# Induced attention and channel mix on one core: the product for the previous token moved onto half of the array's rows

## The chip, the cores and the metric

The kernel runs on one NeuronCore of a Trainium2 chip. The metric is the device time of one execution in microseconds (us). Three runs were taken before the change, and one execution was profiled; the profile gives the span from the first to the last instruction.

## The reference

For each of 4 batches x has 12608 tokens of 128 channels. 32 inducing vectors attend to all tokens of a batch and give h (32 x 128); each token then attends to h. What comes out passes through a channel mix with the previous token:

```python
h = mab(I, x)                # softmax(scale * I x^T) x, per batch
a = mab(x, h)                # softmax(scale * x h^T) h, per token
x_prev = shift(a, 1)         # zeros for the first token
xk = mu_k * a + (1 - mu_k) * x_prev
xr = mu_r * a + (1 - mu_r) * x_prev
k = maximum(xk @ w_k, 0)     # 128 -> 1024
v = k * k @ w_v              # 1024 -> 128
out = sigmoid(xr @ w_r) * v
```

The kernel never forms a. With p the token's 32 attention weights, a @ (mu_k w_k) is p @ (h mu_k w_k): for each batch it folds h, mu and w into two matrices, W0 for the token and W1 for the previous one, of 32 rows and 1024 + 128 columns (the last 128 for the gate w_r). Both p and W are split into a high and a low part that together keep float32's precision in a faster product type. So a row block of 32 partitions of R (p's parts) meets a row block of W0 or W1, and with two parts of each there are four combinations a matrix: 4 x 32 = 128 rows.

## The kernel before, in words

**Units.** Tokens are worked in groups g of 512, 25 a batch (24 full ones and a last of 320). The 1024 columns are eight chunks of 128, worked two at a time: a unit is one group and two chunks, so four units a group, 100 a batch, 400 in all, written as steps n of one loop. In step n the loop writes, in this order: the upward products of unit n (`up`, L773 with W0 and the tokens, L775 with W1 and the tokens shifted by one, both over 128 rows, summed in one of the two two-bank tiles ps_a); the square (`square`: relu to k_t on DVE, L785; the rounded square kh on ACT, L790, or in chosen steps, `high_vector`, on DVE, L787; the square itself on ACT, L791; their difference kl on POOL, L793); in the second unit of a group the gate (`zgate`, L762 and L763, two more products, then a sigmoid on ACT, L765); the downward products of unit n - 4 (`down`, L804: kh with wvh, kh with wvl, kl with wvh, for two chunks). When a group's last unit is done DVE multiplies by the gate (L809), transposes into the output tile ot (L820), and SP issues four stores (L827) for every four groups. ot has one buffer, so its next use waits for the stores.

**R.** R holds p's parts for one group: 128 partitions and 513 columns, column 0 being the last token of the group before. The row blocks are high, low, high, low. It has ten buffers. SP fills it in `spread` (L664): four copies within on-chip memory for a group, each of 32 partitions by 512. Before them `halo` (L587) copies the column for the token before from R of the previous group, as one transfer.

**The work between.** The rest is written into the loop's steps by `at(n, ...)`, in blocks that start every 12 steps. `stage_a(b + 1, j)` prepares the next batch: four DVE transposes of x into tiles xs (three buffers), each followed by four copies into xt on SP (L336, 16 a block), then scores against the inducing vectors (L361), exponentials and a sum (L426), and a load of x (L205). `stage_b(b, j)` makes p for a block of four groups: scores against h (L610), softmax steps on DVE and ACT over some ten steps, the parts ah on ACT (L650) and al on DVE (L654), and then in four steps the four spreads. The last block, the tail of 320 tokens, goes through the same steps with narrower copies. `combine` makes h, its four copies scaled by mu (L519), and W, whose row blocks SP copies (L565, 24 copies a batch).

**Order.** All this is written out by hand: every engine works strictly in program order, and SP too issues its DMAs in the order of the steps, waiting at each for its producers. Batch 0 differs: a head prepares it before the loop, and its first four groups' R are put directly from PSUM, by one ACT copy each (L738).

Of the kernel before, what the change touches and what calls it, by code (L numbers as in the profile page):

```python
# [19 lines left out]
def kernel(  # L20
# [15 lines left out]
    P = 128  # L36
# [8 lines left out]
    LAG = 4  # L45
    NU = FC // UC
# [9 lines left out]
    r_pool = ctx.enter_context(tc.tile_pool(name="r_pool", bufs=10))  # L56
# [23 lines left out]
    wv_sb = mp.tile([P, Q * G], F32, name="ot", bufs=1)[:, :F].rearrange("p (c d) -> p c d", d=C)  # L80

    def load_weight(dst, src, n, raw):
# [11 lines left out]
        def steps():  # L94
# [20 lines left out]
            def sign():  # L115
                X.r = st.tile([P, G], I32, name="aT")[:, :n]
                v.tensor_scalar(out=X.r, in0=hi, scalar1=-2147483648, scalar2=None, op0=ALU.bitwise_and)
# [185 lines left out]
    def xt_tile(S, j, i):  # L303
# [4 lines left out]
        elif i == 0:  # L308
            S.xt_tail = xt_pool.tile([P, TAIL], F32, name="xtl", bufs=1)
# [4 lines left out]
    def stage_a(b, j, at, t):  # L314
# [13 lines left out]
        def btr(c):  # L328
            if c == 0:
                for i in range(Q):  # L330
                    xt_tile(S, j, i)
            xs = st.tile([P, G], F32, name="xs", bufs=3)
            nc.vector.transpose(out=xs.rearrange("p (s q) -> p s q", q=M),  # L333
                                in_=S.xb[j][:, :, M * c:M * (c + 1)])
            for i in range(Q):
                nc.sync.dma_start(out=S.xt[j, i][M * c:M * (c + 1), :], in_=xs[M * i:M * (i + 1)])  # L336
# [70 lines left out]
        def t_etrans():  # L407
            ps = pb_tile("b")
# [36 lines left out]
        for c in range(Q):  # L445
            at(t + (-1, 0, 1, 3)[c], lambda c=c: btr(c))
        if tail:
            at(t + 5, t_tr)
# [20 lines left out]


    def combine(b, at=None, t=0):
# [18 lines left out]
        def weights():  # L490
# [6 lines left out]
            ps = pb_tile(None if ahead else "b")  # L497
# [12 lines left out]
        def hfin():  # L510
            ps = pb_tile(None if ahead else "b")
# [5 lines left out]
            for nm, mu in (("k0", muk), ("k1", omuk), ("r0", mur), ("r1", omur)):  # L517
                h4 = L["h4"][nm] = sm.tile([P, P], F32, name="h4" + nm, bufs=1)
                nc.vector.tensor_scalar(out=h4, in0=h, scalar1=mu, scalar2=None, op0=ALU.mult)  # L519
            S.W = [wp.tile([P, WF], F32R, name=f"W{s}") for s in range(2)]  # L520

        def wpart(s, c, tile):
# [13 lines left out]
            def low():  # L536
                nc.vector.tensor_tensor(out=dst[P // 2:], in0=X["ps"][P // 2:, :],
                                        in1=dst.bitcast(F32)[P // 2:], op=ALU.subtract)
            return prod, high, low

        def wpack(parts, cw, tags, t):
# [33 lines left out]
        at(t + 9, weights)  # L575
        at(t + 10, hfin)
# [490 lines left out]
```

## Time and profile before

| what | value |
|---|---|
| three runs | 1167.78, 1167.95 and 1170.74 us, median 1167.95 |
| the profiled execution | 1165.47 us |
| its span, first to last instruction | 1163.7 us |
| granted TensorE clock | 0.996 of full speed |
| PE, ACT, POOL, DVE busy | 96%, 83%, 81%, 80% of the span |
| DMA | 102.31 MB in 273515 packets, 40.5% of the 16 engines' time on SP's queue |

In the rows that follow, a timeline row gives the start in us, the length in us, the engine (SPq is SP issuing a DMA), the line, what is written from what, and how many instructions were merged. A row of the waits gives the waiting engine and line, whom it waited for, and then us in total, times, and the longest in us. A row of the groups gives the count, busy us, the mean in ns and idle us before. A matmul's end is modelled, so lengths of matmuls overlap: the distance between two starts is the time that one takes.

### The profile page before, as it was taken

The page shows a single profiled execution, that of the slowest core. Times are in us where ns is not written, and L with a number is a line of the kernel's source. Part 1 is how long each engine was busy: PE and PEld are TensorE (multiplying, and loading weights), DVE is VectorE, ACT ScalarE, POOL GpSimd, SP SyncE. Part 2 cuts the span into 40 slices and gives each one's busy share as a digit, 9 for nine tenths or more (in the row PEclk, how much of TensorE's full clock was granted, in tenths as well). Part 3 has the DMA queues.
Part 4 walks back from the last instruction along what each step waited for, and adds up shares of the span by engine and source line. Part 5 has one row for each costly group of instructions (what it writes and reads, how often), then busy time and mean ns, then how long its engine had stood idle before and what let it go on. Part 6 is the DMA issues. An engine that isn't in the chain of part 4 may idle for free.

```text
span 1163.7 us, 17576 instructions
## 1 busy us (share of the span) xinstructions
PE 1114.2 (96%) x5746; PEld 834.2 (72%) x5746; DVE 934.3 (80%) x1259; ACT 970.9 (83%) x1107; POOL 947.7 (81%) x413
## 2 busy tenths in 40 slices
PE   7779999999999999999999999999999999999997
PEld 5456777776677777777767777777768777777886
DVE  5778889887878888888787889897787888887665
ACT  5478888887888888788978988888789888889996
POOL 1158888888787888888879888888878899999997
PEclk9989999999999999999999999999999999999999
DMA  9112554544226455465043554645304314432231
GB/s 288 50 32 75 128 118 106 109 117 92 39 58 134 108 105 123 108 135 120 5 76 74 118 125 104 134 96 124 45 15 82 63 34 73 73 64 46 43 46 34
DMA packets 273515, 102.31 MB, mean 88 GB/s; under 512 B 232816, under 2 KB 248336, under 8 KB 271120
## 3 DMA queue, kind: packets, MB, share of 16 engines
q1 hardware_dynamic: 273088, 101.17, 40.5%
q8 instruction: 46, 0.75, 0.3%
q14 instruction: 45, 0.37, 0.1%
q10 hardware_dynamic: 336, 0.02, 0.0%
HBM read 28.07 MB, written 25.82 MB: 46 GB/s over the span
## 4 chain that ended last, share of the span: by engine, by line
PE 61%; DVE 15%; ACT 8%; SPq 6%; issue 5%; DMA 4%; DVEq 0%; ACTq 0%
PE ps_v L804 31%; PE ps_a L773 11%; PE ps_a L775 10%; DVE k_t L785 5%; SPq L336 2%; DMA out_dram<-ot 2%; ACT kh L790 2%; SPq L827 2%; PE pb_a L426 1%; PE pb_b L610 1%; PE ps_v L762 1%; PE ps_v L763 1%; SPq L664 1%; ACT k_t L791 1%; PE pb_a L361 1%
## 5 line engine op out<-in xcount | busy, mean ns | idle before, releaser
L793 POOL TENSOR_TENSOR kl<-k_t,kh 128x1024 fp32r<-128x1024 f32 (+2 forms) x400 | 939.0, 2375 | 169.0 <-ACT k_t L791 148.9
L785 DVE TENSOR_SCALAR k_t<-ps_a 128x1024 f32<-128x1024 f32 (+1 forms) x400 | 480.9, 1202 | 155.5 <-PE ps_a L775 144.1
L791 ACT ACTIVATE k_t<-k_t 128x1024 f32<-128x1024 f32 (+1 forms) x400 | 418.2, 1048 | 45.5 <-DVE kh L787 34.3
L790 ACT ACTIVATE kh<-k_t 128x1024 fp32r<-128x1024 f32 (+1 forms) x352 | 365.9, 1040 | 104.5 <-DVE k_t L785 57.8
L773 PE MATMUL ps_a<-R,W 128*128 128x512 f32 (+1 forms) x800 | 325.9, 408 | 4.7 <-DMA R<-al 3.4
L775 PE MATMUL ps_a<-R,W 128*128 128x512 f32 (+1 forms) x800 | 313.6, 392 | 0.0
L804 PE MATMUL ps_v<-kh,wvh 128*128 128x512 f32 (+1 forms) x800 | 251.9, 396 | 5.5 <-ACT rT L765 5.0
L804 PE MATMUL ps_v<-kl,wvh 128*128 128x512 f32 (+1 forms) x800 | 249.2, 393 | 0.0
L804 PE MATMUL ps_v<-kh,wvl 128*128 128x512 f32 (+1 forms) x800 | 249.0, 392 | 0.0
L773 PEld LDWEIGHTS ps_a<-R,W 128*128 128x128 f32 x800 | 151.2, 189 | 82.3 <-issue 22.4
L804 PEld LDWEIGHTS ps_v<-kh,wvh 128*128 128x128 f32 x800 | 147.9, 189 | 42.3 <-ACT rT L765 10.1
L804 PEld LDWEIGHTS ps_v<-kl,wvh 128*128 128x128 f32 x800 | 149.6, 188 | 35.5 <-POOL kl L793 0.3
L804 PEld LDWEIGHTS ps_v<-kh,wvl 128*128 128x128 f32 x800 | 149.8, 188 | 34.9
L775 PEld LDWEIGHTS ps_a<-R,W 128*128 128x128 f32 x800 | 151.1, 189 | 29.8
L820 DVE STREAM_TRANSPOSE ot<-oT 128x512 f32<-128x512 f32 x96 | 67.4, 702 | 12.2 <-DMA out_dram<-ot 11.3
L809 DVE TENSOR_TENSOR oT<-ps_v,rT 128x512 f32<-128x512 f32 (+1 forms) x100 | 66.7, 667 | 2.4 <-PE ps_v L804 0.2
L787 DVE SCALAR_TENSOR_TENSOR kh<-ps_a,k_t 128x1024 fp32r<-128x1024 f32 x48 | 58.8, 1225 | 5.4 <-PE ps_v L804 0.5
L765 ACT ACTIVATE rT<-ps_v 128x512 f32<-128x512 f32 (+1 forms) x99 | 57.2, 578 | 0.3
L333 DVE STREAM_TRANSPOSE xs<-xb 128x512 f32<-128x512 f32 x72 | 50.0, 695 | 0.3
L765 ACT ACT_TABLE_LOAD x31 | 39.8, 1283 | 0.6
L762 PE MATMUL ps_v<-R,W 128*128 128x512 f32 (+1 forms) x99 | 38.9, 393 | 0.0
L763 PE MATMUL ps_v<-R,W 128*128 128x512 f32 (+1 forms) x99 | 38.7, 391 | 0.0
(194 smaller groups left out, 643.6 us busy)
## 6 DMA issues: line engine op xcount, KB each, us to landing
out_dram<-ot SPq DMA_DIRECT2D x92, 256.0 KB, 4.4
xb<-in_x_dram SPq DMA_DIRECT2D x18, 1024.0 KB, 5.3
xt<-xs SPq DMA_DIRECT2D x288, 64.0 KB, 2.0
R<-ah SPq DMA_DIRECT2D x184, 64.0 KB, 2.0
R<-al SPq DMA_DIRECT2D x184, 64.0 KB, 2.0
kh<-in_x_dram SPq DMA_DIRECT2D x4, 512.0 KB, 8.2
kl<-in_x_dram SPq DMA_DIRECT2D x4, 512.0 KB, 6.4
xb<-in_x_dram SPq DMA_DIRECT2D x8, 256.0 KB, 5.4
```

Source lines behind the costliest of these rows:

```text
L762: nc.tensor.matmul(out=ps[:, :w], lhsT=S.W[0][:, F:WF], rhs=R[:, 1:w + 1], start=True, stop=False)
L765: nc.scalar.activation(out=self.rT, in_=ps[:, :w], func=AF.Sigmoid)
L773: nc.tensor.matmul(out=ps[:, c, :w], lhsT=S.W[0][:, cs], rhs=R[:, 1:w + 1], start=True, stop=False)
L775: nc.tensor.matmul(out=ps[:, c, :w], lhsT=S.W[1][:, cs], rhs=R[:, 0:w], start=False, stop=True)
L785: nc.vector.tensor_scalar(out=k, in0=self.ps[:, :, :w], scalar1=0.0, scalar2=None, op0=ALU.max)
L787: nc.vector.scalar_tensor_tensor(out=kh, in0=self.ps[:, :, :w], scalar=0.0, in1=k, op0=ALU.max, op1=ALU.mult)
L790: nc.scalar.activation(out=kh, in_=k, func=AF.Square)
L791: nc.scalar.activation(out=k, in_=k, func=AF.Square)
L793: return lambda eng, a, z: eng.tensor_tensor(out=kl[:, :, a:z], in0=k[:, :, a:z], in1=kh.bitcast(F32)[:, :, a:z], op=ALU.subtract)
L804: nc.tensor.matmul(out=self.v, lhsT=wt[:, fc, :], rhs=kk[:, c, :], start=(fc == 0 and n == 0), stop=(fc == FC - 1 and n == 2))
L809: nc.vector.tensor_tensor(out=self.oT, in0=self.v, in1=self.rT, op=ALU.mult)
L820: nc.vector.transpose(out=ot[:, o:o + w], in_=self.oT)
```

## The change

*Products.* One of the four combinations of parts, low with low, is left out for each of the two matrices. The six that remain need 192 rows: 128 for one full product and 64 for a second. The full product has W0's three combinations and, in its last row block, one of W1's with the high part shifted by one column; the half has W1's other two. R becomes [128, 2, 513]: plane 0 for the full product and, in its rows 0 to 63, the half for even chunks; plane 1 in rows 64 to 127 holds the same half for odd chunks. In a unit, both full products come first, then the two halves, one on rows 0 to 63 and one on rows 64 to 127, into different banks. The gate gets a full product and one half alone. Shape, type and count of the downward products stay.

*Copies.* A spread is six copies instead of four, and a halo three transfers instead of one (in the head, three DVE copies instead of one). W keeps 24 copies a batch, three for each part of W0 and five for each of W1. Of the scaled copies of h, two are whole, two cover 96 columns, and two DVE copies fill the rest. The head puts a group's R by two ACT copies and one DVE copy.

*Memory.* R has six buffers of the double width instead of ten; ot holds two groups instead of four, and stores are issued every two groups; the tail's output no longer has a tile of its own; xt of the tail has two buffers.

*Order.* From batch 1 on, blocks start every 14 steps instead of 12, stage_a of the next batch 13 steps ahead of its stage_b; in batch 0 stage_a keeps 12 steps and stage_b has steps of its own. A transpose of x and its copies may stand in different steps. The tail's softmax is written closer together. `combine` and the next batch's first stage_b keep their distances to the last stage_a block (21 and 25 steps from its start). The steps with kh on DVE move, and are 14 a batch from batch 1 on. Some small products use the other PSUM bank.

The diff, cut to its core:

```diff
-    r_pool = ctx.enter_context(tc.tile_pool(name="r_pool", bufs=10))
+    r_pool = ctx.enter_context(tc.tile_pool(name="r_pool", bufs=6))
...
         def btr(c):
+            L["xs", c] = st.tile([P, G], F32, name="xs", bufs=3)
...
+        def bmove(c):
...
             for i in range(Q):
-                nc.sync.dma_start(out=S.xt[j, i][M * c:M * (c + 1), :], in_=xs[M * i:M * (i + 1)])
+                nc.sync.dma_start(out=S.xt[j, i][M * c:M * (c + 1), :], in_=L["xs", c][M * i:M * (i + 1)])
...
-        for c in range(Q):
-            at(t + (-1, 0, 1, 3)[c], lambda c=c: btr(c))
+        for c, n in enumerate((-2, -1, 1, 3) if b > 1 else (-1, 0, 1, 3)):
+            at(t + n, lambda c=c: btr(c))
+            at(t + max(n, -1), lambda c=c: bmove(c))
...
+    W_FIRST = ((0, 0, 0), (0, 1, 0), (0, 2, 1))
+    W_SECOND = ((0, 3, 0), (1, 1, 0), (1, 3, 0), (1, 0, 1), (1, 2, 1))
+    def r_tile():
+        return r_pool.tile([P, UC, G + 1], F32R, name="R")
...
-            for nm, mu in (("k0", muk), ("k1", omuk), ("r0", mur), ("r1", omur)):
-                h4 = L["h4"][nm] = sm.tile([P, P], F32, name="h4" + nm, bufs=1)
-                nc.vector.tensor_scalar(out=h4, in0=h, scalar1=mu, scalar2=None, op0=ALU.mult)
+            for nm, mu, omu in (("k", muk, omuk), ("r", mur, omur)):
...
+                nc.vector.tensor_scalar(out=h1, in0=h, scalar1=omu, scalar2=None, op0=ALU.mult)
...
+                nc.vector.tensor_scalar(out=h0[:, :P - M], in0=h[:, :P - M], scalar1=mu, scalar2=None, op0=ALU.mult)
+                nc.vector.tensor_copy(out=h0[:, P - M:], in_=h1[:, P - M:])
...
-                for q in range(Q):
-                    nc.sync.dma_start(out=S.W[s].bitcast(F32)[M * q:M * (q + 1), c0:c0 + cw],
-                                      in_=X["hl"][q // 2][M * n:M * (n + 1)])
+                for d, q, k in (W_FIRST, W_SECOND)[s]:
+                    nc.sync.dma_start(out=S.W[d].bitcast(F32)[M * q:M * (q + 1), c0:c0 + cw],
+                                      in_=X["hl"][k][M * n:M * (n + 1)])
...
     def halo(S, g, far=True):
...
-        elif far:
-            nc.sync.dma_start(out=S.R[g].bitcast(F32)[:, 0:1], in_=S.R[g - 1].bitcast(F32)[:, G:G + 1])
+        for dst, src in ((R[:half, 0, 0:1], O[:half, 0, G:G + 1]),
+                         (R[half:, 1, 0:1], O[half:, 1, G:G + 1]),
+                         (R[P - M:, 0, 1:2], O[half:P - M, 1, G:G + 1])):
+            if far:
+                nc.sync.dma_start(out=dst, in_=src)
+            else:
+                nc.vector.tensor_copy(out=dst.bitcast(F32R), in_=src)
...
         def spread(i):
...
-            for q in range(Q):
-                nc.sync.dma_start(out=R[M * q:M * (q + 1), 1 + o + lo:1 + o + w],
-                                  in_=src[q % 2][M * i:M * (i + 1), lo:w])
+            for q, h, k, d in ((0, 0, 0, 1), (1, 0, 1, 1), (2, 0, 0, 1), (3, 0, 0, 2), (2, 1, 0, 1), (3, 1, 1, 1)):
+                z = min(w, G + 1 - d - o)
+                nc.sync.dma_start(out=R[M * q:M * (q + 1), h, d + o + lo:d + o + z],
+                                  in_=src[k][M * i:M * (i + 1), lo:z])
...
-                nc.scalar.copy(out=S.R[g][:, 1:G + 1], in_=ps)
+                nc.scalar.copy(out=R[:P - M, 0, 1:G + 1], in_=ps[:P - M])
+                nc.vector.tensor_copy(out=R[P // 2:, 1, 1:G + 1], in_=ps[P // 2:])
+                nc.scalar.copy(out=R[P - M:, 0, 2:G + 1], in_=ps[P // 2:P - M, :G - 1])
...
-            nc.tensor.matmul(out=ps[:, :w], lhsT=S.W[0][:, F:WF], rhs=R[:, 1:w + 1], start=True, stop=False)
-            nc.tensor.matmul(out=ps[:, :w], lhsT=S.W[1][:, F:WF], rhs=R[:, 0:w], start=False, stop=True)
+            nc.tensor.matmul(out=ps[:, :w], lhsT=S.W[0][:, F:WF], rhs=R[:, 0, 1:w + 1], start=True, stop=False)
+            nc.tensor.matmul(out=ps[:, :w], lhsT=S.W[1][:P // 2, F:WF], rhs=R[:P // 2, 0, 0:w],
+                             start=False, stop=True)
...
-            for c in range(UC):
-                cs = slice((u * UC + c) * P, (u * UC + c + 1) * P)
-                nc.tensor.matmul(out=ps[:, c, :w], lhsT=S.W[0][:, cs], rhs=R[:, 1:w + 1],
+            for c, cs in enumerate(cols):
+                nc.tensor.matmul(out=ps[:, c, :w], lhsT=S.W[0][:, cs], rhs=R[:, 0, 1:w + 1],
                                  start=True, stop=False)
-                nc.tensor.matmul(out=ps[:, c, :w], lhsT=S.W[1][:, cs], rhs=R[:, 0:w],
+            for c, cs in enumerate(cols):
+                rows = slice(c * P // UC, (c + 1) * P // UC)
+                nc.tensor.matmul(out=ps[:, c, :w], lhsT=S.W[1][rows, cs], rhs=R[rows, c, 0:w],
                                  start=False, stop=True)
...
-            span = 1 if self.b == B - 1 and g // Q == NBLK - 2 else Q
+            span = 1 if self.b == B - 1 and g // Q == NBLK - 2 else UO
...
-    SEG = 12
...
+        if b == 0:
+            first_a = [t + 3 + 12 * j for j in range(NBLK - 1)]
+            first_b = [t + n for n in (4, 16, 28, 40, 63, 77)]
+            high_vector |= {s + n for s in first_a for n in (4, 8)}
+        else:
+            first_a = [t - 9 + 14 * j for j in range(NBLK - 1)]
+            first_b = [t + n for n in (4, 18, 32, 46, 60, 74)]
+            high_vector |= {s + n for s in first_a for n in (7, 10)} | {t + 80, t + 90}
...
         if b + 1 < B:
-            s = t + SEG * (NBLK - 1)
-            combine(b + 1, at, s)
-            stage_b(b + 1, 0, at, s + 13)
+            s = first_a[-1]
+            combine(b + 1, at, s + 21)
+            stage_b(b + 1, 0, at, s + 25)
```

More of the change, by code (lines that the diff above doesn't have):

```diff
@@ L510, in hfin @@
         def hfin():
-            ps = pb_tile(None if ahead else "b")
+            ps = pb_tile(None if ahead else "a")
             nc.tensor.matmul(out=ps[:, :P], lhsT=S.acc, rhs=L["sw"], start=True, stop=True)
@@ L696, in scores @@
                 del S.xt[0, g]
-                S.R[g] = r_pool.tile([P, G + 1], F32R, name="R")
+                S.R[g] = r_tile()
         def diff():
@@ L838 @@
     order_a = [(b, j) for b in range(B) for j in range(NBLK)]
-    def k_tile():
-        return mp.tile([P, UC * G], F32, name="k_t", bufs=4)
     def halves():
```

98 lines of the change are left out of this document (49 added, 49 removed).

## The prediction

> **What bounds the kernel now.** I read the page first, then the timeline of PE, then that of SP, the queue that issues nearly every DMA.
>
> ```profile
> span 1163.7 us, 17576 instructions
> PE 1114.2 (96%) x5746; PEld 834.2 (72%) x5746; DVE 934.3 (80%) x1259; ACT 970.9 (83%) x1107; POOL 947.7 (81%) x413
> PE 61%; DVE 15%; ACT 8%; SPq 6%; issue 5%; DMA 4%; DVEq 0%; ACTq 0%
> L793 POOL TENSOR_TENSOR kl<-k_t,kh 128x1024 fp32r<-128x1024 f32 (+2 forms) x400 | 939.0, 2375 | 169.0 <-ACT k_t L791 148.9
> ```
>
> PE is busy nearly throughout and carries 61% of the chain that ended last. What a unit (two chunks of one group; four units a group, 100 a batch) costs it is read from start to start, since matmul ends are modelled:
>
> ```profile
> 604.44 0.40 PE L773 MATMUL ps_a<-R,W 128*128 128x512 f32 x1
> 604.67 0.39 PE L775 MATMUL ps_a<-R,W 128*128 128x512 f32 x1
> 604.90 0.63 PE L804 MATMUL ps_v<-kh,wvh 128*128 128x512 f32 x2
> ```
>
> A full 512-column product takes a slot of 0.233 us (604.44, 604.67, 604.90). A unit is four upward and six downward products, ten slots or 2.33 us; a gate of two slots comes once a group. The batches begin with the first upward product of their group 0:
>
> ```profile
> 54.98 0.50 PE L773 MATMUL ps_a<-R,W 128*128 128x512 f32 x1 [0.68 <-ACT R L738]
> 346.25 0.47 PE L773 MATMUL ps_a<-R,W 128*128 128x512 f32 x1 [2.07 <-DMA R<-al]
> 624.82 0.40 PE L773 MATMUL ps_a<-R,W 128*128 128x512 f32 x1
> 902.78 0.39 PE L773 MATMUL ps_a<-R,W 128*128 128x512 f32 x1
> ```
>
> So the four batches last 291.3, 278.6, 278.0 and, to the end of the span, 260.9 us. The first three also prepare the next batch. The second batch begins with PE waiting 2.07 us for a copy into R: SP is not far from mattering already.
>
> **The change part by part.** *Upward products.* If two halves on different rows run side by side, a unit has nine slots instead of ten: 96 full units save 0.233 us and the four 320-column units about 0.146 (0.233 by 320/512), 23 us a batch. PE's batch falls from 278.6 to 256. POOL's next limit is 100 units by 2375 ns, 238 us, so it doesn't end the gain in the first three batches. In the last, 260.9 less 23 would be 238, where POOL's floor alone is met with nothing for start and tail: I allow 8 us there.
>
> *The copies into R.* Here is what else a group pays. SP issues in order, and its rows show the rate:
>
> ```profile
> 490.70 0.51 SPq L587 DMA_DIRECT2D R<-R  x1
> 491.26 0.60 SPq L664 DMA_DIRECT2D R<-ah  x1
> 491.90 0.59 SPq L664 DMA_DIRECT2D R<-al  x1
> 492.53 0.59 SPq L664 DMA_DIRECT2D R<-ah  x1
> 493.17 0.59 SPq L664 DMA_DIRECT2D R<-al  x1
> 493.85 2.44 SPq L336 DMA_DIRECT2D xt<-xs  x4
> 496.45 0.51 SPq L587 DMA_DIRECT2D R<-R  x1
> ```
>
> Queued one behind another, a copy into R or xt takes 0.64 us of SP and a halo 0.56 (490.70 to 491.26). Stores are dearer when longer:
>
> ```profile
> 502.82 4.52 SPq L827 DMA_DIRECT2D out_dram<-ot  x4
> 1140.88 1.96 SPq L827 DMA_DIRECT2D out_dram<-ot  x4
> ```
>
> Four stores of a four-group span take 4.5 us, four of a one-group span 2.0; for two groups I take 2.8, between them and nearer the smaller.
>
> SP's work in one of the first three batches, before: six blocks of 16 spreads and 16 for the tail, 112 by 0.64, 72 us; 24 halos, 13; 96 copies into xt, 61; 24 into W at the same price, 15; stores, six times 4.5 and once 2.0, 29; seven loads at 0.55, 4. Together 194 of 279 us, 70%. After: 6 spreads a group, 24 groups and 24 for the tail, 168 by 0.64, 107; three halos a group, 72 by 0.56, 40; xt 61; W 15, 24 copies still though ordered 3 and 5; stores 13 by 2.8, 36; loads 4. Together 263 us. That passes PE's 256.
>
> *The halo's wait.* A halo reads the end of the group before, so it waits until that group's copies have landed:
>
> ```profile
> 936.71 0.59 SPq L664 DMA_DIRECT2D R<-al  x1
> 938.83 0.51 SPq L587 DMA_DIRECT2D R<-R  x1
> ```
>
> The last copy was issued by 937.30, the halo began at 938.83: 1.53 us in which SP does nothing, behind it all copies, stores and loads. Of three halos, the first reads rows copied first and can go; the second waits, 1.53 less the first's 0.56, say 1.0 us. Before, copies into xt often stood between. With blocks of 14 steps the four spreads follow each other directly, so three of a block's four groups pay: 18 a batch, 18 us. With it SP needs 281 us a batch. The bounds are 0 (other transfers between) and 1.5 a group (27 us); I take the middle one because it follows from the order of rows.
>
> *Who waits for SP when it is late.* PE, for R; and DVE, in order, for its tiles:
>
> ```profile
> DVE ot L820 <- DMA out_dram<-ot: 11.3, 6, 2.7
> SPq L664 <- ACT ah L650: 57.2, 13, 12.4
> SPq L664 <- DVE al L654: 44.9, 19, 3.9
> SPq L827 <- DVE ot L820: 102.1, 14, 21.7
> ```
>
> The output tile has one buffer and now turns over every second group, 12 times a batch rather than 6. The transpose that opens it waits for the stores, and behind it on DVE stand the next k_t, oT and token stage. At 11.3/6 = 1.9 us, all 36 turns of three batches would hold DVE 68 us. The L664 rows are SP waiting for its own producers, 102 us over four batches. Even a full queue must wait for some of them: I take a quarter, 25 us, as time lost to SP for either cause; bounds 0 and 68.
>
> *Small things.* The four scaled copies of h become four scalings and two copies:
>
> ```profile
> 309.39 2.42 DVE L519 TENSOR_SCALAR h4k<-hT,omuk 128x128 f32<-128x128 f32 x1
> 311.74 2.42 DVE L519 TENSOR_SCALAR h4r<-hT,mur 128x128 f32<-128x128 f32 x1
> ```
>
> Of four, two took 2.42 us. Two more instructions cost DVE at most 4.8 us a batch, 15 in all; the two ps_a buffers cover about one unit, and when SP is late PE isn't what waits, so I count nothing, with up to 15 in the range. A head group's R is put by two ACT copies and a DVE copy for one ACT copy, on the path only for group 0: under 1 us. The moved transposes, banks, k_t squares and tail steps add no work; they can only shift a wait, within the bounds above. Ten R buffers become six of double width, so a spread may not start before the group six earlier is used; at 14 steps a block that allows a lead of under two blocks, the reason why a late SP cannot be paid from stock.
>
> **The sum.** SP's steady work begins with batch 1's first transposes:
>
> ```profile
> 71.55 15.94 SPq L336 DMA_DIRECT2D xt<-xs  x16
> ```
>
> 71.6 + 3 x 281 = 914.6, plus 25 lost, is 939.6, when the last batch can start (902.78 before). It then takes 260.9 - 8 = 253: a span of 1192.5. The profiled execution has 1165.5 for a span of 1163.7, so 1.8 more, 1194. The median of the runs, 1167.95, is 2.5 above the profiled execution; half of that is within the runs' scatter, and I forecast **1195 us**: PE's saving is real, and SP takes it back and a little more. Without the 25 it would be 914.6 + 253 + 1.8 = 1169, without the halos' 54 too 1115; with all at their worst, beside the 1195, (27 more for the halos, 43 more for DVE) about 1265; likely for this case is 1160 to 1230.
>
> *A rule on issuing.* The 0.64 us between starts decides this. The Trainium skill, "DMA: Bandwidth & Descriptors", in its table of where the fixed 2 us goes, gives a dispatch by the sequencer about 50 ns, and calls issue time usually small beside the transfer. By that, some 390 issues a batch would be an estimated 20 us and SP no limit, the first rival below. The trace disagrees: 0.64.
>
> **The rivals.** *Faster: SP doesn't bind.* If halos find their data landed and stores go at the one-group price, SP needs 263 - 10 = 253 us a batch, under PE's 256. Then PE sets the pace: 54.98 + (291.3 - 23) + 2 x 256 + 253 + 2 = 1090, and with R late by some 7 us at each batch's start **1110 us**. The point that decides is 256 us of SP a batch. For it: SP now spends 204 us waiting in the three rows above alone, so it has room. Against: those waits are where it is early, and the start-to-start rows are steady.
>
> *Slower: a switch of the array's shape.* The trace has no 64-row product. The nearest are the token stage's 32-column ones, between full ones:
>
> ```profile
> 112.38 0.63 PE L804 MATMUL ps_v<-kl,wvh 128*128 128x512 f32 x2
> 112.93 1.07 PE L610 MATMUL pb_b<-xt,hT 128*32 128x512 f32 x8
> 113.93 0.50 PE L773 MATMUL ps_a<-R,W 128*128 128x512 f32 x1
> 114.27 0.40 PE L775 MATMUL ps_a<-R,W 128*128 128x512 f32 x1
> ```
>
> Two slots after 112.38 is 112.85; the narrow ones start at 112.93, 0.08 late. After them the first full product holds 0.34 us instead of 0.233: its weights weren't loaded ahead, 0.11. If halves pay the same both ways, with 128 columns of weights each time, a unit pays 2 x (0.08 + 0.11) = 0.38 to save 0.233, a loss of 0.15; a gate, whose lone half saves nothing, pays 0.38. 400 x 0.15 + 100 x 0.38 = 98 us, and with R still late at the starts **1270 us**. For it: every narrow group shows it. Against: narrow columns need separate data paths for the moving rows; rows may not, and no row here tells.
>
> The Trainium skill, "TensorEngine Tiling (Array Packing)", Key Properties, says that changing the tiling mode, not just the tile, drains TensorE. By that rule this rival holds for rows too. The trace agrees for columns (0.08).
>
> *The halves run one after the other.* Then PE keeps its ten slots, 279 us, beside SP's 281: neither can catch up, and some 10 us more is lost at each batch's start: **1225 us**. For it: nothing but that no row shows row halves; against: the eight narrow products above start within 1.07 us in all.
>
> **How the numbers follow.** A measurement here can tell 0.3% (3.5 us) from no change. SP sets the pace: 0.42 (of it 0.07 faster, 0.08 the same, 0.27 slower). SP doesn't bind: 0.27, faster. The switch: 0.23, slower. One after the other: 0.08, slower. Together 0.34 faster, 0.08 the same, 0.58 slower. The range 1120 to 1275 leaves out the lower half of the fast rival and the top of the slow one.
>
> **What would show it.** Right: pairs of half products starting within some 20 ns, a slot of 0.233 for both; SP issuing without a gap over most of 100 to 900 us, with R waits of several us on PE at the batch starts (steps 0 and 16 of a batch) and DVE's wait for stores well over 11.3 us; the last batch starting near 940. Wrong: R waits under 5 us in all and batches of 260 us (the fast rival); a first half that starts over 0.3 us after the second full product, and a long first down product (the switch); halves 0.23 us apart.

## The result, and the profile after

After the change the kernel takes 1339.28 us (median of four runs, 1334.93 to 1340.22), before it 1168.28 beside it on the same chip: a ratio of 1.1452, 95% interval 1.1421 to 1.1482. The profiled execution took 1339.95 us. The forecast was 1195, at most 1275: the sign was right, and the size was a sixth of the true one.

The page of the kernel after, the rows that answer to those of before:

```profile
span 1338.2 us, 18413 instructions
PE 1246.8 (93%) x5746; PEld 747.4 (56%) x5746; DVE 936.9 (70%) x1290; ACT 981.8 (73%) x1109; POOL 947.2 (71%) x413
PEclk9889998989989998998999789999899999999999
PE 68%; SPq 9%; DVE 5%; DMA 5%; issue 2%; ACT 2%; DVEq 0%; ACTq 0%
```

DVE, ACT and POOL have nearly the work they had. PE has 133 us more of it (by modelled ends), although the change was to take work from it, and SP's issuing (SPq) is 9% of the chain instead of 6%. The clock, 0.996 over the run before, is 0.963.

The timeline of PE, one unit and then the stretch around a gate:

```profile
600.36 0.62 PE L801 MATMUL ps_a<-R,W 128*128 128x512 f32 x2
600.91 0.50 PE L805 MATMUL ps_a<-R,W 64*128 64x512 f32 x2
601.35 0.73 PE L834 MATMUL ps_v<-kh,wvh 128*128 128x512 f32 x2
...
602.85 0.40 PE L801 MATMUL ps_a<-R,W 128*128 128x512 f32 x1
...
608.83 0.50 PE L789 MATMUL ps_v<-R,W 128*128 128x512 f32 x1
609.26 0.50 PE L790 MATMUL ps_v<-R,W 64*128 64x512 f32 x1
609.70 0.72 PE L834 MATMUL ps_v<-kh,wvh 128*128 128x512 f32 x2
```

The halves (L805) do run side by side: the median distance between the starts of a pair is 3 ns. But two full products from 600.36 would end their slots at 600.83, and the pair starts at 600.91, 0.08 late. After it the next product waits until 601.35, 0.44 later, where a slot is 0.233, and the six down products take 1.50 us, where six slots are 1.40. The unit lasts 2.49 us (600.36 to 602.85) instead of 2.33, and a gate 0.87 (608.83 to 609.70) instead of 0.47. That is the prediction's rival of the switch, in size too: it had worked out losses of 0.15 a unit and 0.38 a gate, and these are 0.16 and 0.40.

The first upward products of the four batches:

```profile
58.52 0.73 PE L801 MATMUL ps_a<-R,W 128*128 128x512 f32 x2 [2.01 <-ACT R L765]
404.99 0.40 PE L801 MATMUL ps_a<-R,W 128*128 128x512 f32 x1
718.43 0.64 PE L801 MATMUL ps_a<-R,W 128*128 128x512 f32 x2
1045.27 0.64 PE L801 MATMUL ps_a<-R,W 128*128 128x512 f32 x2
```

The batches last 346.5, 313.4, 326.8 and, to the end, 292.9 us, against 291.3, 278.6, 278.0 and 260.9. The loss is in all of them (55, 35, 49 and 32 us), and larger in the three beside which the next batch is prepared.

The waits of the kernel after:

```profile
PEld ps_a L805 <- issue: 144.2, 386, 0.7
PEld ps_v L834 <- issue: 73.2, 298, 0.4
PEld ps_a L801 <- DVE k_t L815: 35.3, 17, 6.4
DVE ot L848 <- DMA out_dram<-ot: 29.3, 11, 6.8
DVE xs L331 <- DMA xt<-xs: 25.9, 8, 7.2
DVE xs L331 <- DMA xb<-in_x_dram: 23.3, 2, 13.5
PE ps_a L801 <- DMA R<-ah: 11.5, 4, 3.0
```

The first two are the switch, seen from the weight loads: on 386 occasions the load of a half's weights had nothing to wait for that the profile shows, and still was not done ahead, and so with the first down product behind it. The rest comes from the queue. PE seldom waits for R itself (11.5 us). What comes late from SP holds DVE, at the output tile, at the tiles xs and at a load of x, and PE waits for the k_t behind that. One such place in the timelines of SP, DVE and PE:

```profile
736.78 0.58 SPq L206 DMA_DIRECT2D xb<-in_x_dram  x1
...
742.64 0.71 DVE L331 STREAM_TRANSPOSE xs<-xb 128x512 f32<-128x512 f32 x1 [13.49 <-DMA xb<-in_x_dram]
743.27 0.45 DVE L839 TENSOR_TENSOR oT<-ps_v,rT 128x320 f32<-128x320 f32 x1
743.65 1.21 DVE L815 TENSOR_SCALAR k_t<-ps_a 128x1024 f32<-128x1024 f32 x1
...
743.78 0.79 PE L789 MATMUL ps_v<-R,W 128*128 128x512 f32 x1 [10.45 <-DVE oT L839]
```

SP issues a load of x only at 736.78, behind a row of copies and halos. DVE's transpose of it stands ahead of oT and k_t and is held for 13.49 us; PE has nothing for 10.45. The same stretch by the table of windows (window, its length, then the busy times of PE, PEld, DVE, ACT and POOL with counts, granted clock, DMA share, GB/s):

```profile
717.00:732.00 15.00, 15.00 (x76) 8.96 (x76) 9.40 (x12) 10.07 (x12) 13.12 (x7) 1.00 0.24 54
732.00:748.00 16.00, 5.55 (x17) 3.25 (x14) 5.33 (x8) 2.77 (x3) 3.16 (x3) 0.63 0.64 147
748.00:755.00 7.00, 7.00 (x26) 4.11 (x25) 4.79 (x7) 5.71 (x7) 5.58 (x3) 0.88 0.34 70
...
744.00:748.00 4.00, 4.00 (x9) 2.54 (x10) 3.97 (x6) 2.77 (x3) 0.77 (x1) 0.50 0.59 121
```

The granted clock is 1.00 before the stall, 0.63 over the stall and the first 4 us of work behind it, and 0.88 in the next 7 us. In those first 4 us alone (744 to 748), with PE busy throughout, it is 0.50: PE pays for a long stall a second time, with slow products after it. The trace has 16 stretches at half clock, 102 us in all, where the kernel before has two, 12 us. Half of PE's busy time in them is an estimate of what PE loses this way: 40 us, against 2.5 before.

### The profile page after: what moved, and what is told of

Read it like the earlier page. It is cut to its first block, busy times and chain, and to the rows that moved or that the text cites. A ratio compares the mean times of both kernels' runs of the same rounds, so it can differ in the third digit from the quotient of the medians.

```text
span 1338.2 us, 18413 instructions
## 1 busy us (share of the span) xinstructions
PE 1246.8 (93%) x5746; PEld 747.4 (56%) x5746; DVE 936.9 (70%) x1290; ACT 981.8 (73%) x1109; POOL 947.2 (71%) x413
## 4 chain that ended last, share of the span: by engine, by line
PE 68%; SPq 9%; DVE 5%; DMA 5%; issue 2%; ACT 2%; DVEq 0%; ACTq 0%
PE ps_v L834 36%; PE ps_a L801 12%; PE ps_a L805 10%; SPq L693 5%; DVE k_t L815 3%; PE ps_v L790 3%; PE ps_v L789 3%; PE pb_b L638 1%; DMA R<-al 1%; PE pb_a L364 1%; SPq L585 1%; SPq L339 1%; DMA out_dram<-ot 1%; PE pb_a L429 1%; SPq L855 1%
## 5 line engine op out<-in xcount | busy, mean ns | idle before, releaser
L801 PE MATMUL ps_a<-R,W 128*128 128x512 f32 (+1 forms) x800 | 270.0, 419 | 44.8 <-DVE k_t L815 26.1
L834 PE MATMUL ps_v<-kh,wvh 128*128 128x512 f32 (+1 forms) x800 | 296.2, 452 | 0.4 <-ACT rT L793 0.4
L801 PEld LDWEIGHTS ps_a<-R,W 128*128 128x128 f32 x800 | 145.3, 194 | 122.3 <-issue 37.9
L805 PE MATMUL ps_a<-R,W 64*128 64x512 f32 (+1 forms) x800 | 203.5, 501 | 0.2 <-DMA R<-al 0.2
L834 PEld LDWEIGHTS ps_v<-kh,wvh 128*128 128x128 f32 x800 | 121.9, 192 | 93.8 <-issue 73.2
L805 PEld LDWEIGHTS ps_a<-R,W 64*128 64x128 f32 x800 | 76.6, 186 | 150.7 <-issue 144.2
L848 DVE STREAM_TRANSPOSE ot<-oT 128x512 f32<-128x512 f32 (+1 forms) x100 | 69.3, 693 | 29.5 <-DMA out_dram<-ot 29.3
L817 DVE SCALAR_TENSOR_TENSOR kh<-ps_a,k_t 128x1024 fp32r<-128x1024 f32 (+1 forms) x54 | 64.9, 1203 | 10.5 <-PE ps_v L834 6.2
L789 PE MATMUL ps_v<-R,W 128*128 128x512 f32 (+1 forms) x99 | 49.8, 503 | 11.7 <-DVE oT L839 11.7
L790 PE MATMUL ps_v<-R,W 64*128 64x512 f32 (+1 forms) x99 | 49.8, 503 | 0.0
```

Of the source, the lines that this page charges most:

```text
L789: nc.tensor.matmul(out=ps[:, :w], lhsT=S.W[0][:, F:WF], rhs=R[:, 0, 1:w + 1], start=True, stop=False)
L790: nc.tensor.matmul(out=ps[:, :w], lhsT=S.W[1][:P // 2, F:WF], rhs=R[:P // 2, 0, 0:w], start=False, stop=True)
L801: nc.tensor.matmul(out=ps[:, c, :w], lhsT=S.W[0][:, cs], rhs=R[:, 0, 1:w + 1], start=True, stop=False)
L805: nc.tensor.matmul(out=ps[:, c, :w], lhsT=S.W[1][rows, cs], rhs=R[rows, c, 0:w], start=False, stop=True)
L834: nc.tensor.matmul(out=self.v, lhsT=wt[:, fc, :], rhs=kk[:, c, :], start=(fc == 0 and n == 0), stop=(fc == FC - 1 and n == 2))
L848: nc.vector.transpose(out=ot[:, o:o + w], in_=self.oT)
```

## The experiments

Two theories stood at first. A: the switch of the array's shape and the late queue both cost, and add up. B: the queue alone, with halves that gain what they promise. Some of the kernels don't compute the reference's sums: the halves in the kernel before leave out rows, and the kernel after with full rows takes in rows of other data. In all of them the count, size and shape of the other products stay. Ratios are to the kernel before on the same chip (1169 to 1170 us in each set).

**The halves alone, in the kernel before.**

```diff
             for c in range(UC):
                 matmul(ps[:, c, :w], S.W[0][:, cs], R[:, 1:w + 1])
-                matmul(ps[:, c, :w], S.W[1][:, cs], R[:, 0:w])
+            for c in range(UC):                 # rows 0-63 or 64-127; the gate: rows 0-63
+                matmul(ps[:, c, :w], S.W[1][rows, cs], R[rows, 0:w])
```

> The kernel before with one edit: the second upward product of each chunk and of the gate takes 64 rows instead of 128, even chunks on rows 0 to 63, odd chunks on rows 64 to 127, both full products first and then both halves. R, W, all copies, stores and steps stay as before; the other 64 rows of the previous token's matrix are left out of the sums. Theory A (the change of the array's row shape costs PE some 0.16 us net in each unit and 0.40 us in each gate, as the timeline of the changed kernel shows from start to start: 600.36 to 602.85 is 2.49 us for a unit instead of 2.33, and 608.83 to 609.70 is 0.87 us for a gate instead of 0.47): 400 x 0.16 + 100 x 0.40 = 104 us more than before, about 1270 us, with a unit of 2.49 us where nothing else waits. Theory B (the DMA queue alone is what slows the changed kernel, and the switch lies in time that PE would have waited anyway): the copies are as before, so a slot less in each unit makes it faster, 1080 to 1140 us.

1243.91 us, ratio 1.0639 (1.0608 to 1.067), at a clock of 0.995. The queue is untouched, so the switch alone costs 74 us. B's gain isn't there. The 74 us are less than the 104 that 0.16 a unit and 0.40 a gate would make: some of it, it seems, falls where PE was waiting anyway.

**The gate's second product full again.** As before, with the gate's half taken back:

> The kernel before with halves in the upward products, as in the run of the halves alone (1244), but the gate's second product over all 128 rows again; it too leaves out 64 rows of the previous token's matrix in the upward products. Theory A (each change of shape costs by itself, and the gate's lone half pays 0.38 to 0.40 us a group with nothing saved): 100 gates give 38 to 40 us back, 1204 to 1210. Theory U (only the unit's switch is on the path; the gate's is covered by the narrow products and waits near it): 1235 to 1244.

1207.7 us, ratio 1.0329 (1.0288 to 1.037). The gate's hundred lone halves cost 36 us, which is 0.36 each, and the 400 units the other 39, which is 0.10 each of the 0.16 in the rows. So it is the units whose cost is partly covered.

**Two pairs of switches a unit instead of one**: full, half, full, half.

> As the first of these four kernels, but in the old order: full, half, full, half, so that the array's row shape changes four times in a unit instead of twice and the halves of two chunks never run together. Theory A, from the distances in the timeline of the changed kernel (full to half 0.32, half to the next full 0.44, a full one after a switch 0.43 to the next switch, and 0.11 more in the first down product): 0.32 + 0.44 + 0.43 + 0.44 + 0.11 = 1.74 us from the first full to the first down product instead of 0.93, 0.81 us a unit and 0.40 a gate: 364 us over the kernel before, about 1530 us. Theory B: four slots as before and no other cost, about 1168 us.

1484.55 us, ratio 1.2697 (1.2639 to 1.2756), another 241 us or 0.60 a unit (the rows had given 0.81, about 1530 us). The timeline of PE shows why:

```profile
699.60 0.49 PE L776 MATMUL ps_a<-R,W 64*128 64x512 f32 x1
700.02 0.49 PE L773 MATMUL ps_a<-R,W 128*128 128x512 f32 x1
700.44 0.50 PE L776 MATMUL ps_a<-R,W 64*128 64x512 f32 x1
700.87 0.49 PE L762 MATMUL ps_v<-R,W 128*128 128x512 f32 x1
```

With the shape changing at each product, a product takes 0.42 us (699.60, 700.02, 700.44, 700.87), 0.19 over its slot, and no half runs beside another. The Trainium skill, "TensorEngine Tiling (Array Packing)", Key Properties, says that changing the tiling mode drains TensorE. These rows agree, for 64-row tiles, with 0.19 us a change.

**The change without the switch.** The kernel after, with the second product over all 128 rows:

```diff
-                matmul(ps[:, c, :w], S.W[1][rows, cs], R[rows, c, 0:w])
+                matmul(ps[:, c, :w], S.W[1][:, cs], R[:, 0, 0:w])
```

> The changed kernel with one edit: the second upward product of a chunk and of the gate takes all 128 rows of plane 0 again, so no product changes the array's row shape except the token stage's; the halo's first transfer covers 128 partitions instead of 64. All copies, stores and steps stay as changed; the sums get rows that the reference doesn't have. Theory A: the 104 us of the switch go, and what the queue costs by itself stays: 1339 - 104 = about 1235 us, that is some 65 us over the kernel before, with PE waiting for R and for k_t. Theory B: the queue sets the pace whatever PE does, so it stays within 30 us of 1339 us. A third reading, C (the queue's lateness only hurts because PE is already late, through idle time and the lower clock after it): it falls to 1170 to 1195 us.

1311.9 us, ratio 1.1221 (1.1188 to 1.1253). Only 27 us come off. So the rest of the change costs 142 us by itself, far above A's price of some 65, and A's adding up falls: 74 and 142 are more than the 171 of both. B's figure for this run holds (within 30 us of 1339). The queue sets the pace most of the time and hides a good part of the switch. The waits, with the switch's two lines gone:

```profile
PE ps_a L801 <- DVE k_t L814: 59.0, 18, 7.9
DVE ot L847 <- DMA out_dram<-ot: 43.6, 15, 8.0
DVE xs L331 <- DMA xt<-xs: 41.4, 8, 8.6
DVE xs L331 <- DMA xb<-in_x_dram: 26.8, 4, 13.7
PE ps_a L801 <- DMA R<-ah: 18.5, 5, 5.3
```

**The halos taken off SP.** The kernel after, with the three halo transfers as small DVE copies one or two units ahead:

```diff
-                halo(S, j * Q + i)              # in spread: three DMAs on SP
+                if j * Q + i == 0: halo(S, 0)
...
+            halo(nxt.S, nxt.g, far=False)       # in the loop: three DVE copies
```

> The changed kernel with the halo columns copied by DVE (three small copies a group, one or two units before the group is used) instead of by three transfers on SP; everything else as changed. It frees SP of 72 x 0.56 = 40 us a batch and of the wait for the landing of the copies before (41 us in 54 waits over the whole run). Theory A: only the queue's part of the loss goes, 40 to 65 of the 172 us: 1275 to 1300 us, and the unit stays at 2.49 us. Theory B: most of the loss goes, 1150 to 1200 us.

1275.63 us, ratio 1.0911 (1.0879 to 1.0942): 64 us come back for 279 transfers of 256 bytes or less, and the clock is 0.986. That is what A gave here (1275 to 1300); B's 1150 to 1200 isn't reached. So neither theory stands as a whole: the queue costs more than A said, and the switch more than B. The same without the switch:

> The kernel after with both repairs at once: the second product over all 128 rows (no change of the array's shape) and the halos as small DVE copies (no halo on SP's queue). The extra rows that the second product reads belong to other data, so the sum of the previous token's parts is not the reference's. Left of the change on SP: six copies a group instead of four, stores every two groups, blocks of 14 steps, six R buffers. Theory H (the three halos, each waiting for the copies before it, are the whole of the queue's 142 us): within 15 us of the kernel before, 1160 to 1185, with DVE's waits for transfers (ot, xs) gone. Theory C (copies and small stores carry a good part by themselves): 1215 to 1260, with SP waiting little and DVE still held by ot. By adding up (1276 for the kernel after without halos, less the 74 that the halves cost alone) it would be 1202.

1210.97 us, ratio 1.0357 (1.0315 to 1.0399). It lies between H and C, near the sum of the parts. The halos are 101 us of the 142, and 42 are something else.

**The small stores alone, in the kernel before.**

```diff
-    ot = tile([P, Q * G]);  stores when g % Q == Q - 1
+    ot = tile([P, 2 * G]);  stores when g % 2 == 1
```

> The kernel before with the output tile of two groups and stores every two groups: the part of the change on stores alone, all of the computation kept. Theory S (the one output tile turns twice as often and each turn holds DVE for the stores, 1.9 us or more): 18 to 24 turns more at 1.9 us and up hold DVE some 45 us, and the time rises by 20 to 60. Theory N (a turn waits only where SP is late already, and SP has some 30% of room here): within 5 us of the kernel before, DVE's wait for stores under 25 us.

1162.59 us, ratio 0.9945 (0.9922 to 0.9967): not slower but faster, by half a per cent. S falls, and so does the forecast's view of the output tile as a cost in itself: DVE's wait for stores there is 2.0 us in all, where it was 11.3. In this kernel, where SP has room, a turn of the tile costs nothing.

**Is it late transfers, or SP's time?** The loads of x, and then the stores too, issued by ACT in the kernel after with full rows:

```diff
-            nc.sync.dma_start(out=t, in_=x[b, ...])
+            nc.scalar.dma_start(out=t, in_=x[b, ...])
```

> The kernel after with the second product over all 128 rows (1311.9, no change of shape; the sum of the previous token's parts takes in rows of other data, as there), and the loads of x for the next batches issued by ACT instead of SP. SP keeps everything else, so its work falls by 4 of some 274 us a batch. In the run with full rows DVE waited 26.8 us in 4 waits for such a load that SP had issued late, the longest 13.7, and one step lasted 15.9 us. Theory H (a transfer that is late holds DVE at an instruction ahead of its k_t, and PE behind that): the 27 us go, and some of the time at half clock that follows such a stall: 1265 to 1287, the longest step under 10 us. Rival W (SP is late by its own work all the same, and the time goes to the next wait): 1295 to 1315.

1338.73 us, ratio 1.1451 (1.1431 to 1.1471), 27 slower than with the loads on SP, and outside what either theory gave. H falls: DVE's wait for the load left the list, and its wait for the stores grew from 43.6 to 69.7. The stall of 13 us is where the lateness shows and not where it arises. Why it is even slower isn't settled, and W, which gave at most 1315, isn't confirmed by it.

> The same with the stores too issued by ACT: SP then has copies into R, xt and W and three halos a group, some 238 us of issue a batch instead of 274, and no longer waits for the output tile (70 us over three batches) with copies queued behind it. Theory Q (what counts is SP's issue and waits together against PE's 280 us a batch): 1200 to 1235, halos and all, as in the run without halos on SP (225 us a batch, 1211). Theory D (the halos cost by themselves: each waits for its copies to land, some 35 waits, and PE gets R late whatever else SP does): above 1265. Theory T (ACT, in order, is held at each issue for the output tile's transpose and pays some 0.6 us for each of 52 x 4 stores, 125 us, and becomes late itself): also above 1265, but with ACT waiting for DVE's ot and PE waiting for ACT.

1323.51 us, ratio 1.1321 (1.1301 to 1.1341). SP is relieved and nothing is gained over the 1311.9 with full rows, but ACT is late now, as T said, though in other waits than T named:

```profile
DVE e L408 <- ACT e1t L397: 50.1, 15, 8.0
ACT kh L819 <- DMA R<-R: 42.4, 6, 8.6
ACT kh L819 <- DMA out_dram<-ot: 33.1, 6, 12.9
```

So this run says nothing for or against Q. The question was put more cleanly: in the run without halos on SP, give SP their issue time back and nothing else.

```diff
+                for p0, p1 in ((0, 64), (64, 128), (96, 128)):
+                    nc.sync.dma_start(out=spare[p0:p1, k:k + 1], in_=muk[p0:p1])
```

> The kernel after with full rows and the halos by DVE (1211), and, where each group's three halo transfers stood on SP, three transfers of the same small shapes from a constant into a spare tile that nothing reads and nothing waits for. They take SP's issue time, some 40 us a batch, and wait for nothing. Theory I (the halos cost by their issue time: SP's issue, its small gaps and its waits together come to the batch's length, so each us added to SP is added to the batch): 1290 to 1320, most of the 100 us back. Theory W (the halos cost by waiting for the copies of the group before, with the queue held behind them): 1208 to 1235.

1314.59 us, ratio 1.1226 (1.1149 to 1.1302): 104 us are back, and so all of the 101, by transfers that nobody waits for. Three of them and what stands around them, in SP's timeline:

```profile
483.44 3.50 SPq L341 DMA_DIRECT2D xt<-xs  x4
487.04 0.53 SPq L208 DMA_DIRECT2D xb<-in_x_dram  x1
487.61 1.77 SPq L694 DMA_DIRECT2D spare<-muk  x3
```

A transfer of 64 x 4 bytes holds SP for 0.59 us (1.77 for three), as long as a copy of 32 x 2 KB. The tiny transfers don't slow the others on their way: the copies into R land 2.0 us after their issue (median of the page) in the kernels with them and without. And the other side, the halos on SP but behind their own group's copies, where they need not wait:

> The kernel after with full rows (1311.9), each group's halos on SP still, but issued behind the six copies of their own group instead of ahead of them, so that the copies of the group before have landed by then: some 3.8 us later, against a wait of 1 us or more now. The number of transfers and their issue time are the same. Theory W: 1215 to 1260, SP's waits at the halo's line gone. Theory I: 1290 to 1312; the 23 us that SP waited there over three batches may come off, no more.

1308.12 us, ratio 1.117 (1.1099 to 1.1242). I holds and W falls: the halo's wait for data is worth next to nothing, its issue time nearly everything. The sums over SP's single issues, from its first copy into xt for batch 1 (71.4 to 73.5 us) to the start of the last batch, three batches together, in us (issue; gaps up to 0.35 us between issues; longer gaps, in which it waits):

| kernel | issue | small gaps | waits | stretch |
|---|---|---|---|---|
| before | 560 | 51 | 221 | 831 |
| full rows, halos by DVE | 612 | 57 | 205 | 874 |
| the same and idle transfers | 761 | 67 | 133 | 961 |
| full rows | 728 | 73 | 157 | 957 |
| full rows, halos behind copies | 740 | 66 | 152 | 958 |
| after | 725 | 69 | 180 | 973 |

The merged rows of the timeline hide part of these waits: the three halos at 403.74 further down take 2.48 us as one row, with the wait for a copy's landing inside. The idle transfers put 159 us more of issue and gaps on SP. Of these, 72 come out of its waits, and 87 lengthen the stretch; another 19 lie in the last batch (283.0 us for 264.4). So I's "each us added to SP is added to the batch" holds for a good half. Part of what SP's lateness costs comes through the clock: PE's loss at half clock, by the estimate used above, is 17 us with full rows and halos by DVE, 46 with the idle transfers and 43 with full rows alone.

None of these kernels brings the waits below 133 us. They are SP's own, for producers that aren't ready when their turn in its order comes: in the stretch of the kernel after, the largest are

```profile
SPq L855 <- DVE ot L848: 73.8, 10, 17.5
SPq L615 <- DMA R<-al: 30.3, 39, 2.6
SPq L339 <- DVE xs L331: 27.0, 10, 7.9
```

In the run with the halos behind, the waits ahead of a halo fall from 28 us to 10, and the total only from 157 to 152: SP then waits longer elsewhere.

**What is left, 42 us.** Without halos on SP, the steps before group 4 of a batch are long, and PE waits for R there. The first block of batches 1 to 3 begun two steps earlier:

```diff
-            first_b = [t + n for n in (4, 18, 32, 46, 60, 74)]
+            first_b = [t + n for n in (2, 18, 32, 46, 60, 74)]
```

> The kernel after with full rows and halos by DVE (1211) and, from batch 1 on, the first block of the token stage two steps earlier in a batch, so that R of group 4 is begun four steps ahead of its use instead of two; the other blocks stay. There the steps 115 and 215, the last before group 4, lasted 7.8 and 8.8 us, and the ones behind them 4.8 and 4.6. Theory L (what is left of the change, 42 us, is in good part R's short lead at the batch starts): steps 115 and 215 under 4 us, 1190 to 1202. Rival (the lead is set by the queue and not by the step, as blocks follow each other): 1206 to 1214.

1196.53 us, ratio 1.0235 (1.0213 to 1.0256). PE's upward products, without the edit and then with it:

```profile
407.30 0.74 PE L802 MATMUL ps_a<-R,W 128*128 128x512 f32 x2
415.07 1.19 PE L802 MATMUL ps_a<-R,W 128*128 128x512 f32 x2 [5.16 <-DMA R<-ah]
```

```profile
407.56 0.63 PE L802 MATMUL ps_a<-R,W 128*128 128x512 f32 x2
410.99 0.73 PE L802 MATMUL ps_a<-R,W 128*128 128x512 f32 x2
```

The step of 7.8 us is gone; L holds, with 14 of the 42 us. The change's own order had left group 4's R two steps of lead. And in the kernel after itself, with its halves:

> The kernel after, with its halves and all of its computation, the halos by DVE (1275.6), and the first block of a batch two steps earlier as in the run that fell from 1211 to 1196.5. Theory L (R's short lead counts with the change of shape as without it): 1255 to 1266, so that what is left over the halves alone in the kernel before (1243.9) is 11 to 22. Rival (the change of shape makes the steps longer, and in us the lead is enough): 1271 to 1280.

1266.21 us, ratio 1.0812 (1.0764 to 1.0861), 0.2 above the upper end of what L gave: 9 us of the 14 come off here too. Compared with the run above it, the switch is worth 70 us once the queue is out of the way, as it is (74) in the kernel before.

**A version better than both.** The kernel before with its one halo a group as a DVE copy:

> The kernel before with its one halo a group as a small DVE copy a unit or two ahead instead of a transfer on SP; all of the computation kept. Theory R (the queue is late already at the batch starts, where PE waits some 2 us for R): 1158 to 1165, a version better than both. Theory E (PE carries the time, and the queue has room, so its relief buys nothing): within 0.3% of the kernel before; the copies cost DVE some 0.1 us a group, 10 us in all, beside other work.

1160.33 us, ratio 0.992 (0.989 to 0.995), 9 us better than before. With the two-group stores as well:

> The kernel before with both edits that made it faster by themselves: halos as a small DVE copy, and an output tile of two groups with stores every two groups; all of the computation kept. If the two savings (9 and 6.5 us) add up: 1152 to 1156. If both take away the same wait (R late at a few steps, SP late behind a long store): 1157 to 1161, no better than the halos alone.

1161.6 us, ratio 0.9932 (0.9917 to 0.9946): the two savings don't add up. They seem to take away the same wait: DVE's waits for the stores, 11.3 us before, are 2.0 with the small stores alone and 1.4 with the halo moved alone.

## Why the prediction was wrong, point by point

*Upward products: wrong.* "If two halves on different rows run side by side, a unit has nine slots" took the saving as whole and put the change of shape at nothing. They do run side by side; the saving is there and the switch takes it back with 0.16 more. The rival had the mechanism and its size right, to 0.01 us a unit and 0.02 a gate. It had a chance of 0.23, and the rows for columns bore on rows better than the text allowed ("narrow columns need separate data paths").

*The copies into R: right.* 263 us of SP a batch were forecast; issue and small gaps come to 794 / 3 = 265. The price of 0.64 a copy holds. Three halos that need not wait took 1.85, 0.62 each with 0.56 forecast, and four two-group stores 2.5, with 2.8 forecast:

```profile
403.74 2.48 SPq L615 DMA_DIRECT2D R<-R  x3
406.26 0.58 SPq L693 DMA_DIRECT2D R<-ah  x1
416.63 2.48 SPq L855 DMA_DIRECT2D out_dram<-ot  x4
419.21 1.85 SPq L615 DMA_DIRECT2D R<-R  x3
```

That issue time is a limit at all was a step the forecast took rightly: the idle transfers show 0.59 us each, and 104 us of the kernel's time by them. (Its "some 390 issues a batch" are 419 by its own counts.) The dispatch of about 50 ns, in the Trainium skill, "DMA: Bandwidth & Descriptors", "Anatomy of one DMA — SWDGE (gpsimd) path", stands in a table on the path through GpSimd, so it was no price for SP's queue.

*The halo's wait: too dear, and beside the point.* 18 us a batch were forecast, 30.3 / 3 = 10 measured (the wait for R<-al at L615), and the run with halos behind shows that without most of this wait others take its place.

*Who waits for SP when it is late: the step that failed.* It took 25 us over three batches for SP's waits on its producers and for DVE's on SP, "a quarter" of the 102 us of two rows, when all of SP's waits in the kernel before come to 221. With the 54 for halos that made 79 us of waits; 180 were measured (157 without the switch), and none of these kernels came under 133. A queue whose order is fixed didn't use all its time: the 221 us of waits shrank to 133 when SP was fullest. By these sums, as an estimate, SP becomes the bound not at 256 us of work a batch but some 44 below. The text also looked for the harm in the output tile's turns (68 us at most; 29.3 measured, and in the kernel before more turns cost nothing), and had no term for the tiles xs and the loads of x (49 us of DVE's waits together), nor for the half clock behind long stalls (an estimated 40 us of PE's time).

*The sum.* The last batch starts at 1045.3 instead of 939.6. Of these 106 us 101 are waits (180 for 79), and 5 are issue and gaps (794 for 3 x 263). It then takes 292.9 instead of 253: the halves alone, in the kernel before, made that batch 283.5 (958.6 to 1242.1) from 260.9, the rest of the change without them 281.1 (1029.5 to 1310.7). 106 and 40 are the 146 us by which the profiled execution misses the forecast's 1194.

*The rivals were taken as either-or.* The switch and the slow queue are both true, and the forecast gave each its chance without the time of both together. Taken down in steps, the 1339 us are: 64 for the halos on SP (1276), 9 for the short lead (1266), 70 for the switch (1197), and 27 that remain over the kernel before. The shares hold for this order of steps alone: with the switch taken out first they are 27 for it, 101 for the halos, 14 for the lead and the same 27. The 27 (33 by the profiled executions) are for the most part in batch 0 (310 us from 58.8 to 369.0, against 291.3). One place of it can be read in the kernel that took 1197, in the window from 325 to 360 us:

```profile
DVE xs L331 <- DMA W<-xs: 7.7, 1, 7.7
PE ps_a L802 <- DVE k_t L815: 7.4, 1, 7.4
```

The transposes of x that now stand ahead of batch 1 use the tiles xs, through which the gate's part of W goes at that time; DVE waits for its copies, and PE behind DVE (step 92 lasts 9.9 us). In the kernel before, no such wait is in the list. No run took it away, and which other part of the changed order makes the rest wasn't tried.

*The signs named.* Pairs within 20 ns: seen, but not the slot of 0.233 for both. "A first half that starts over 0.3 us after the second full product, and a long first down product": seen, the switch (0.32 by its slot, 600.59 to 600.91). SP without a gap: not seen, though it was the bound; that sign was wrong, for the reason above. R waits at the batch starts: seen at step 16 of each batch, 2.8 to 3.0 us, and not at step 0. DVE's wait for stores well over 11.3: seen, 29.3. The last batch near 940: not seen, 1045. Of the signs of the fast rival (batches of 260 us) and of halves one after the other (0.23 us apart) neither was seen.

## What to carry to other kernels

A product of another row shape pays at its entry and its exit, here 0.4 us a pair of switches to save 0.233: count switches before slots. For an in-order queue, the waits that stay must be kept in the sum: here at least 44 us of 320 a batch stayed however full it was, so it was the bound at 86% busy, and a sign of "no gaps" missed it. Here a transfer of 256 bytes cost the issuing queue as much as one of 64 KB; an engine with room should make such copies, and where two slow-downs are likely, work out the time of both at once.

## What the runs showed of the hardware that was not expected

Two 64-row products on different rows start 3 ns apart, and still the pair costs 0.44 us to the next full product; alternating shapes make each product 0.42 us instead of 0.233. After a stall of PE such as the 10.45 us above, the granted clock was 0.50 for the next 4 us and more. With 22 stretches at half clock, 127 us in all, its mean was 0.952 with full rows against 0.996 before, with as many products of the same shapes. And a transfer of 64 x 4 bytes took SP 0.59 us.
